# Block-sparse attention with a Fourier-mixing MLP: the first pair in two halves, and the last variances by ScalarE squares

## The chip, the cores and the metric

The kernel runs on one core of one Trainium2 chip. The metric is the device time of one execution in microseconds (us). A core has five engines that run side by side and hand work to each other through semaphores: TensorE (PE in the profile, with its weight loads as PEld), VectorE (DVE), ScalarE (ACT), GpSimd (POOL) and SyncE (SP), which here only issues transfers. Each engine works through its own list of instructions strictly in the order written. Matrix products land in PSUM; DVE and ACT carry them from there to SBUF.

## What is computed

Four batches, eight heads, 768 positions, head size 64. Attention first, in which a query sees its own block of 64 keys and the three blocks with the best gate scores; then a Fourier mix, a layer norm and an MLP over the 512 channels:

```
k_rep = k.reshape(B, H, n_blocks, 64, D).mean(axis=3)
gate_scores = einsum('bhsd,bhnd->bhsn', q, k_rep)        # causal blocks only
top_idx = argsort(gate_scores)[..., -3:]                 # plus the own block
scores = where(mask & causal, q @ k.T / sqrt(D), -1e9)
attn_out = softmax(scores) @ v
x = attn_out as (B, S, 512)
u = x + real(fft(fft(x, axis=1), axis=2))
mu, var = mean(u, -1), mean((u - mu) ** 2, -1)
un = (u - mu) / sqrt(var + 1e-06)
out = u + maximum(un @ w_ch1, 0) @ w_ch2
```

## The kernel before

Heads are taken in pairs: pair P (0 to 15) holds two heads, four pairs make a batch b (0 to 3). The order of all the work is written out by hand in one long string, ORDER. Each word of it is a step: its name, what it works on, and after an @ the number of the buffer slot that it allocates (for matrix products one of a few PSUM slots). A leading ~ moves a step to its second engine. Since the schedule is manual, each engine executes its instructions exactly in this order, and a step that waits holds back all that stands behind it on its engine.

The steps of a pair that matter here:

- Lq, Lk, Lv: the transfers of q, k, v from HBM, issued by SP. Pair 0's q and k are not in ORDER: consts_first issues them, one head on SP's queue, the other on ACT's.
- tq, tk: TensorE turns q and k, 128 positions at a time (a_tp, six transposes; for k of pair 0 four, and tj, b_tp, the other two). qc (a_q32) copies the turned q to SBUF in float32; qs (a_q) and kc (a_k) write the float16 copies that the scores use; ks (a_sums) adds up k over each block of 64.
- g, then gt, gu, gx, go, gl, gm: the gate scores and, on DVE, the top three of them and the mask. Pair 0 has a second set for the last 256 queries (gj, tg, xg, og, lg, mg), so that its first 512 can go ahead.
- s:P,i (s_mm): tile i of the scores; the mask is added by further matmuls at its end. e:P,i (s_exp): the exponential on ACT; d:P,i (s_sel): the causal edge on POOL. v: the product with v; x: its normalization into x_b on DVE.

The steps of a batch: the fold and the Fourier products (fs, fd, f, fe, y, ty, tr, m), then u:b,kp (m_u) on DVE, which adds x, writes two row tiles of u and their row sums into sm. For batches 2 and 3 (W7) follow bn:b,kt (n_stats: two DVE instructions per row tile give its mean and variance), nv:b,kp (n_guess: four small DVE instructions, a first guess of 1/sqrt(var) and the shift), xu:b,kp (m_x: one row tile scaled on DVE, the other on ACT, into x_b) and un:b,kp (t_copy: two transposing transfers, issued by SP, into unT). nr (n_newton, POOL) refines the guess for later use. w:b,it (w1_mm) is the first MLP product, whose first matmul reads columns 0 to 511 of unT; r its relu; c (w2_mm) the second product of batches 0 and 1, and T, S, p, po a seven-product form of it for batches 2 and 3. o and od finish and store a row tile.

At the very start consts_first also runs eight matmuls over a tile of zeros (warmps), before the first transposes.

Of the kernel before, what the change touches and what calls it, by code (L numbers as in the profile page):

```python
# [11 lines left out]
FP = mybir.dt.float32  # L12
F16 = mybir.dt.float16
# [99 lines left out]
d:0,1 Lk:5@2 s:1,3@0 gl:2 s:1,5@3 ~qs:4 tk:4@1 gt:3 gm:2@2 e:1,3 ~gu:3 v:0@2 d:1,4 ks:4 e:1,5 gx:3
kc:4 s:2,3@0 vc:1 go:3 x:0 s:2,0@3 e:2,3@0 Lv:3@0 s:2,4@1 d:1,5 d:1,3 e:2,0 g:4@2 gl:3 d:2,3 fs:0,1
Lv:2@1 tq:5@0 fs:0,0 e:2,4 gm:3@3 d:2,0 Lk:7@0 gt:4 d:1,0 tk:5@3 d:1,2 ~qc:5@1 d:1,1 s:2,5@2 ~kc:5
s:2,1@1 d:2,4 e:2,5 s:2,2@0 ~gu:4 e:2,1 vc:3 ks:5 v:1@2 e:2,2 qs:5 gx:4 s:3,5@1 go:4 s:3,0@3 gl:4
e:3,5@1 d:2,2 x:1 s:3,2@0 e:3,0 Lq:6@0 d:3,5 g:5@1 vc:2 e:3,2 s:3,3@2 gt:5 Lk:6@1 d:2,1 gm:4@0
s:3,1@3 d:3,0 gu:5 s:3,4@1 e:3,3 gx:5 d:2,5 v:2@0 d:3,2 kb:7 LT:0 e:3,1 W:0 Lq:7@1 fs:1,0 ~go:5
e:3,4 s:4,4@2 x:2 d:3,1 s:4,2@3 d:3,3 e:4,4@0 s:4,0@1 d:3,4 gl:5 v:3@0 fs:2,0 gm:5@1 e:4,2 fs:2,1
fs:1,1 e:4,0 s:5,2@2 x:3 s:4,5@3 e:5,2@1 s:4,1@1 fd:2,1 s:4,3@0 fs:3,0 e:4,5 s:5,3@2 fs:3,1 e:4,1  # L120
fd:2,0 s:5,5@3 fd:3,1 e:5,5 tq:6@1 fd:3,0 e:4,3 ~fe:0,3 s:5,0@3 f:0,2 e:5,3 tk:6@0 ~fe:0,0 ~fe:0,2
f:0,0 ~qc:6@0 s:5,4@2 LF:0 f:0,1 fe:0,1 ks:6 e:5,4 y:0,0@1 qs:6 Lv:4@0 f:0,3 e:5,0 Lc:0 pg:0 ks:7
d:4,0 g:6@2 d:4,1 ty:0,0 d:4,2 y:0,1@3 gt:6 Lv:5@1 d:4,5 ~tr:0,0 d:5,2 gu:6 gx:6 Lk:8@2 d:4,3
s:5,1@2 W:1 go:6 gl:6 ~tr:0,1 qc:7@1 m:0,2@1 vc:4 ty:0,1 gm:6@2 d:4,4 kc:6 m:0,0@3 d:5,0 u:0,2@0
d:5,4 e:5,1 Lk:9@1 d:5,3 v:4@0 qs:7 u:0,0@1 xu:0,2 s:6,4@1 xv:0,2 x:4 vc:5 m:0,1@2 kh:7 e:6,4@0
d:5,5 s:6,1@3 u:0,1@2 d:5,1 s:6,3@0 e:6,1 xt:0,2@1 ~xu:0,0 g:7@2 xv:0,0 ~xu:0,1 v:5@3 e:6,3 gt:7
un:0,2 ~gu:7 W:2 ~xv:0,1 xt:0,0@2 s:6,5@1 un:0,0 xt:0,1@0 e:6,5 s:6,0@1 un:0,1 Lq:9@2 s:6,2@2 e:6,0
x:5 w:0,8@0 d:6,0 bn:0,0 w:0,1@1 r:0,8 gx:7 kc:7 go:7 w:0,5@3 gl:7 gm:7@3 K:7 kb:8 w:0,6@0 r:0,5
ks:8 r:0,1 bn:0,3 w:0,3@3 r:0,6 d:6,3 bn:0,5 e:6,2 w:0,12@1 r:0,3 Lq:8@0 s:7,5@0 s:7,0@2 ~r:0,12
e:7,5@1 s:7,4@3 kh:8 e:7,0 s:7,3@0 fs:4,1 w:0,0@1 qc:9@0 e:7,4 Li:0 Lv:6@0 kb:9 e:7,3 w:0,10@2 qs:9  # L130
Lv:7@1 bn:0,1 r:0,0 s:7,1@3 Lk:10@0 r:0,10 ks:9 d:7,3 w:0,11@0 e:7,1 qc:8@1 s:7,2@1 kh:9 ~r:0,11
d:7,1 w:0,7@2 e:7,2 d:6,2 d:7,0 fs:5,1 d:6,4 ~qs:8 g:8@3 X:0 g:9@0 gt:8 w:0,14@1 gu:8 d:7,4 gx:8
r:0,7 d:6,5 ~go:8 kc:9 w:0,9@3 X:1 gl:8 gt:9 gu:9 gm:8@0 d:6,1 d:7,5 w:0,2@2 r:0,14 ~r:0,9 Lk:12@1
d:7,2 vc:7 ~vc:6 gx:9 w:0,13@0 K:8 kc:8 kb:10 w:0,4@1 ~r:0,13 r:0,2 ks:10 v:7@3 r:0,4 ~go:9 gl:9
gm:9@1 K:9 s:8,3@0 x:7 s:8,1@2 v:6@1 e:8,1@1 bn:0,2 e:8,3 s:8,0@3 x:6 d:8,1 w:0,15@2 e:8,0 fs:5,0
fs:6,1 s:9,4@0 fs:7,1 r:0,15 fs:7,0 s:8,2@1 fs:4,0 s:8,4@3 e:9,4@0 fd:7,1 c:0,0,0@2 fs:6,0 fd:6,0
# [60 lines left out]
def kernel(  # L197
# [34 lines left out]
    def pick(a, b):  # L232
        return b if other[0] else a
# [778 lines left out]
```

## Time and profile before

| | us |
|---|---|
| median of 3 runs (277.49 to 278.82) | 277.71 |
| the profiled execution | 277.79 |
| its span | 276.1 |
| TensorE busy | 267.9 |
| VectorE busy | 221.5 |
| ScalarE busy | 178.3 |
| GpSimd busy | 107.4 |

The span is what the trace covers; 1.7 us of the profiled execution lie around it. A row of the timeline gives the start, the duration, the engine, the line of the kernel, the operation, output <- inputs, the shapes and a count; in brackets stands how long the engine had been idle, and what released it. A row with a count above one is a run of instructions without a gap, from the start of the first to the end of the last. "SPq" and "ACTq" are the queues of transfers that SP and ACT issue; the duration there is that of the issue, not of the transfer. A row of the windows gives, for a stretch of time, the busy time of each engine in it. Matmuls overlap in the pipeline, so that a row of the timeline reaches past the start of the next one.

### The profile page before, as it was taken

To read this page: it belongs to the slowest core of one execution; us is meant where nothing else is said; L and a number is where in the kernel's file an instruction comes from. 1 tells how busy PE (TensorE), PEld (TensorE's weight loads), DVE (VectorE), ACT (ScalarE), POOL (GpSimd) and SP (SyncE) were. 2 spreads that over 40 slices of the span, in tenths; PEclk is the share of its full clock that TensorE was granted. 3 is DMA by queue.
4 is the path that set the end of the run, shared out by engine and by line. 5 is a ranking of instruction groups with operands and counts; after the bars stand their busy time and mean duration, and the time that the engine had idled before them with its cause. 6 is when DMAs were issued, how large, how long until landed. Compare 5 with 4: busy or idle time off the path is not lost.

```text
span 276.1 us, 7004 instructions
## 1 busy us (share of the span) xinstructions
PE 267.9 (97%) x2660; PEld 181.2 (66%) x2660; DVE 221.5 (80%) x683; ACT 178.3 (65%) x243; POOL 107.4 (39%) x304
## 2 busy tenths in 40 slices
PE   8899989999999999999999999999999999999995
PEld 4566766765576565666665755655766888666884
DVE  1888999998789889899789797879999894307883
ACT  3799999969999759978799687802546310274100
POOL 5155927634783476405976691520100011000000
PEclk9999999999999999999999999999999999999999
DMA  8999999998799999479471202351100412300025
GB/s 190 271 229 235 186 233 207 180 153 151 134 174 189 168 188 194 115 124 234 119 149 29 57 2 78 77 105 51 38 2 0 59 19 68 127 0 2 0 112 194
DMA packets 121138, 33.47 MB, mean 121 GB/s; under 512 B 113616, under 2 KB 118160, under 8 KB 121104
## 3 DMA queue, kind: packets, MB, share of 16 engines
q1 hardware_dynamic: 115872, 28.43, 48.1%
q0 software_dynamic: 3664, 4.19, 9.8%
q10 hardware_dynamic: 1568, 0.39, 0.6%
q8 instruction: 21, 0.34, 0.5%
q14 instruction: 13, 0.11, 0.1%
HBM read 28.55 MB, written 6.29 MB: 126 GB/s over the span
## 4 chain that ended last, share of the span: by engine, by line
PE 81%; DVE 6%; ACT 5%; POOL 2%; issue 2%; SPq 2%; DMA 1%; DVEq 0%; ACTq 0%; POOLq 0%
PE h L801 19%; PE cw L879 13%; PE c L820 12%; PE h L803 9%; PE sc L532 7%; PE av L567 5%; PE tp L320 2%; ACT pt L549 2%; PE yp L639 2%; PE sc L527 2%; PE mx L672 2%; SPq L742 2%; PE mx L673 2%; PE sc L539 1%; PE warmps L914 1%
## 5 line engine op out<-in xcount | busy, mean ns | idle before, releaser
L549 ACT ACTIVATE pt<-sc 128x1024 f16<-128x1024 f32 (+1 forms) x96 | 83.4, 925 | 12.1 <-PE sc L532 8.1
L801 PE MATMUL h<-unT,w 128*128 128x512 f16 x256 | 84.6, 379 | 0.3 <-DMA unT<-x 0.3
L803 PE MATMUL h<-unT,w 128*128 128x256 f16 x256 | 69.7, 272 | 0.0
L813 ACT ACTIVATE hT<-h 128x768 f16<-128x768 f32 x50 | 39.4, 811 | 41.1 <-PE h L803 40.7
L555 POOL TENSOR_SCALAR_AFFINE_SELECT pt<-pt 128x256 f16<-128x256 f16 x96 | 37.4, 413 | 21.0 <-ACT pt L549 19.9
L820 PE MATMUL c<-w_sb,hT 128*128 128x512 f16 x192 | 44.5, 379 | 0.0
L801 PEld LDWEIGHTS <-w 128*128 128x128 f16 x256 | 25.0, 98 | 29.7 <-issue 1.4
L820 PEld LDWEIGHTS <-hT 128*128 128x128 f16 x192 | 18.3, 98 | 20.3 <-issue 0.5
L253 POOL TENSOR_SCALAR_AFFINE_SELECT qk<-mt 32x160 f16<-32x160 f16 x72 | 23.9, 353 | 18.2 <-DVE mt L504 16.7
L803 PEld LDWEIGHTS <-w 128*128 128x128 f16 x256 | 25.0, 98 | 3.6
L532 PE MATMUL sc<-qk 96*128 96x512 f16 (+3 forms) x144 | 26.1, 305 | 0.0
L567 PEld LDWEIGHTS <-pt 128*128 128x128 f16 x672 | 22.3, 97 | 3.2 <-ACT pt L549 0.7
L567 PE MATMUL av<-v,pt 128*128 128x65 f16 x672 | 23.2, 193 | 0.3 <-ACT pt L549 0.3
L253 POOL TENSOR_SCALAR_AFFINE_SELECT qk<-q 64x768 f16<-64x768 f32 (+1 forms) x15 | 12.3, 822 | 22.8 <-ACT q L239 15.3
L886 DVE SCALAR_TENSOR_TENSOR u<-cw,rt,u 128x256 f32<-128x256 f32 x35 | 16.6, 480 | 4.7 <-PE cw L879 4.1
L879 PEld LDWEIGHTS <-s 128*128 128x128 f16 x192 | 18.8, 98 | 2.2
L532 PEld LDWEIGHTS <-qk 96*128 96x128 f16 x144 | 13.1, 98 | 7.8
L811 DVE TENSOR_SCALAR hT<-h 128x768 f16<-128x768 f32 x14 | 13.3, 956 | 4.0 <-PE h L803 3.9
L879 PE MATMUL cw<-w2t,s 128*128 128x256 f16 x144 | 16.4, 273 | 0.0
L250 DVE TENSOR_TENSOR s<-hT,hT 128x384 f16<-128x384 f16 x16 | 5.4, 354 | 13.4 <-ACT hT L813 13.3
L250 DVE TENSOR_TENSOR x<-av,rcp 128x768 f16<-128x768 f32 x16 | 15.3, 958 | 0.6
L879 PEld LDWEIGHTS <-hT 128*128 128x128 f16 x144 | 14.1, 98 | 2.0
(155 smaller groups left out, 457.2 us busy)
## 6 DMA issues: line engine op xcount, KB each, us to landing
nat<-in_v_dram SPq DMA_DIRECT2D x16, 384.0 KB, 4.6
out_dram<-u SPq DMA_DIRECT2D x20, 256.0 KB, 2.4
nat<-in_k_dram SPq DMA_DIRECT2D x36, 96.0 KB, 3.4
nat<-in_q_dram SPq DMA_DIRECT2D x36, 96.0 KB, 2.9
nat<-in_q_dram SPq DMA_DIRECT2D x13, 192.0 KB, 3.7
nat<-in_k_dram SPq DMA_DIRECT2D x13, 192.0 KB, 3.9
w_sb<-in_moe_w_ch_dram POOLq DMA_DIRECT2D x2, 1024.0 KB, 11.2
w<-in_moe_w_ch_dram POOLq DMA_DIRECT2D x2, 768.0 KB, 7.1
```

Of the source, the lines that this page charges most:

```text
L250: (eng or nc.vector).tensor_tensor(out=out, in0=in0, in1=in1, op=op)
L253: nc.gpsimd.affine_select(out=out, in_=in_, pattern=[[0, i] for i in n], base=0, channel_multiplier=0, compare_op=ALU.is_ge, fill=0.0)
L532: nc.tensor.matmul(ps[:, e, co:co + q1 - q0], qk[0:96, e, 1, 128 * jt:128 * jt + 128], qk[0:96, e, 0, q0:q1], start=True, stop=True)
L549: nc.scalar.activation(out=d["pt"][:, o:o + 2 * n].rearrange("p (e c) -> p e c", e=2), in_=d["sc", i][:, :, 0:n], func=AF.Exp, scale=0.125)
L555: nc.gpsimd.affine_select(out=dg, in_=dg, pattern=[[0, 2], [1, 128]], base=0, channel_multiplier=-1, compare_op=ALU.is_ge, fill=0.0)
L567: nc.tensor.matmul(av[:, e, 66 * st:66 * st + 65], pt[:, co:co + 128], vv[:, e, jt, 0:65], start=(cnt == 0), stop=(cnt == 20))
L801: nc.tensor.matmul(hp[:, 0:512], w1s, unT[:, dt, 0:512], start=(dt == 0), stop=(dt == NDT - 1))
L803: nc.tensor.matmul(hp[:, 512:768], w1s, unT[:, dt, 512:768], start=(dt == 0), stop=(dt == NDT - 1))
L813: nc.scalar.activation(out=hT, in_=hp, func=AF.Relu)
L820: nc.tensor.matmul(c_ps[b, g[0]][:, st - g[0], :], h_t[b, it][:, 128 * st:128 * (st + 1)], w2_sb[:, it, :], start=(it == 0), stop=(it == N ...
L879: nc.tensor.matmul(o, x, y, start=(i == 0 and W7_FIRST[n]), stop=(i == 7), skip_group_check=True)
L886: nc.vector.scalar_tensor_tensor(out=o, in0=c_ps[b, "w", st][:, W7_BANK[n], 0:256], scalar=rt_t[b][:, kt:kt + 1], in1=o, op0=ALU.mult, op1 ...
```

## The change

Start of the kernel:

- The loads of pair 0 go in two parts, rows 0 to 511 and rows 512 to 767, and k ahead of q. The four transfers of the first part are spread over SP and ACT as before, the four of the second part are all issued by SP.
- tq:0 now turns four row tiles; a new step tn:0 (b_tq) turns the other two. The float32 copy is split into ~qc:0 and ~qn:0 (b_q32), both on ACT; the float16 copy into qs:0, now on POOL, and ~qm:0 (b_q) on ACT.
- The zeros are a tile of their own, 128 wide, and are set first; seven warm-up matmuls instead of eight read it, four times over.
- TensorE's order for pairs 0 and 1 was "tq:0 tk:0 tj:0 g:0 gj:0 tq:1 tk:1 s:0,5 s:0,2 s:0,4 g:1 s:0,1 s:0,0 tk:2". It is now "tk:0 tq:0 tj:0 g:0 tn:0 gj:0 s:0,0 tk:1 s:0,2 tq:1 s:0,5 s:0,4 g:1 s:0,1 tk:2".
- DVE finishes the gate of the first 512 queries (gt gu gx go gl gm) before that of the last 256 (tg xg og lg mg); the two were interleaved. On ACT e:0,0 stands first of the exponentials, ahead of ~qc:1; it stood last of the first five, behind it. SP loads k of pair 1 before its q.

Batches 2 and 3: the six bn steps of each are gone. mn:b,kp (n_mean, DVE, one small instruction) turns the row sums into minus the mean, and sq:b,kt (n_square, ACT) squares a row tile of u with that as bias, and adds up the squares; its 512 results go into x_b, where xu overwrites them. nv takes the variance from these sums. On ACT the squares of batch 2 stand thus: "kc:15 sq:2,0 e:14,0 sq:2,4 e:14,1 sq:2,1 sq:2,5 e:14,2 e:14,4 ~vc:14 e:15,5 e:15,0 xu:2,2 e:15,3 e:14,3 xu:2,0 e:14,5 e:15,1 sq:2,2 e:15,2 sq:2,3 e:15,4 xu:2,1".

Elsewhere each engine has its steps in the order of before; many steps have other buffer slots.

```
-        two = P == 0 and who == 1
+        two = P == 0
...
+    def b_tq(P):
+        pairs[P]["tpn"] = ps = pst([128, 256], f"tpn_{P}")
+        src = nat[P, 0].rearrange("p st e d -> p st (e d)")
+        for st in range(4, NST):
+            nc.tensor.transpose(ps[:, 128 * st - 512:128 * st - 384], src[:, st, :], id32)
+
+    def b_q32(P):
+        conv(pick(nc.vector, nc.scalar), q_tile(P)[:, 512:S], pairs[P]["tpn"], None)
+
+    def b_q(P):
+        conv(pick(nc.gpsimd, nc.scalar), qk_s[P % NSLOT][:, 0, XW(P), 512:S], q_tile(P)[:, 512:S], [S - 512])
...
+    def n_mean(b, kp):
+        sm = st_t[b][2][:, 2 * kp:2 * kp + 2]
+        nc.vector.tensor_scalar(out=sm, in0=sm, scalar1=-1.0 / DM, scalar2=None, op0=ALU.mult)
+
+    def n_square(b, kt):
+        nc.scalar.activation(out=x_t[b][:, kt, :], in_=u_t[b, kt // 2][:, kt % 2, :], func=AF.Square,
+                             bias=st_t[b][2][:, kt:kt + 1], accum_out=st_t[b][0][:, kt, 1:2])
...
-            nc.vector.tensor_scalar(out=vr, in0=mv[:, :, 1], scalar1=1e-6, scalar2=None, op0=ALU.add)
+            nc.vector.tensor_scalar(out=vr, in0=ss, scalar1=1.0 / DM, scalar2=1e-6, op0=ALU.mult, op1=ALU.add)
...
-            nc.vector.scalar_tensor_tensor(out=nm, in0=mv[:, :, 0], scalar=-1.0, in1=g,
-                                           op0=ALU.mult, op1=ALU.mult)
+            tt(nm, nm, g, ALU.mult)
...
-        for who in (0, 1):
-            src = (q, k)[who]
-            t = npool.tile([128, NST, 2, 64], FP, tag=f"nat{who}{place[0]}", name=f"nat{who}_0", bufs=1)
-            nat[0, who] = t
-            for e, eng in ((0, nc.sync), (1, nc.scalar)):
-                eng.dma_start(t[:, :, e, :], src[0, e].rearrange("(st p) d -> p st d", p=128))
...
+        for h in (slice(0, 4), slice(4, NST)):
+            for who in (1, 0):
+                src = (q, k)[who]
+                for e, eng in ((0, nc.sync), (1, nc.sync if h.start else nc.scalar)):
+                    eng.dma_start(nat[0, who][:, h, e, :],
+                                  src[0, e].rearrange("(st p) d -> p st d", p=128)[:, h, :])
...
+        nc.vector.memset(wsrc, 0.0)
         nc.vector.memset(dummy, 1.0)
         nc.scalar.activation(out=dummy, in_=dummy, func=AF.Exp)
-        nc.vector.memset(wsrc, 0.0)
         wps = pst([128, 512], "warmps")
-        for _ in range(8):
-            nc.tensor.matmul(wps, wsrc[:, 0:128], wsrc, start=True, stop=True)
-        nc.vector.tensor_copy(out=dummy, in_=wps[:, 0:1])
-        nc.vector.tensor_copy(out=id16, in_=id32)
+        for _ in range(7):
+            nc.tensor.matmul(wps.rearrange("p (r c) -> p r c", c=128), wsrc, wsrc.rearrange(
+                "p (r c) -> p r c", r=1).to_broadcast([128, 4, 128]), start=True, stop=True)
```

More of the change, by code (lines that the diff above doesn't have):

```diff
@@ L113 @@
[L113 to L124, printed above, removed]
@@ new lines @@
+s:7,0@0 ~r:0,12 e:7,5@1 s:7,4@3 kh:8 e:7,0 s:7,3@1 fs:4,1 Li:0 qc:9@0 w:0,0@2 e:7,4 Lv:6@0 kb:9
+qs:9 Lv:7@1 e:7,3 w:0,10@0 bn:0,1 r:0,0 Lk:10@0 d:7,3 ks:9 s:7,1@3 r:0,10 w:0,11@1 qc:8@1 e:7,1
+s:7,2@2 kh:9 ~r:0,11 d:7,1 w:0,7@0 e:7,2 d:6,2 d:7,0 fs:5,1 d:6,4 ~qs:8 g:8@3 X:0 g:9@1 gt:8
+w:0,14@2 gu:8 d:7,4 gx:8 r:0,7 d:6,5 ~go:8 kc:9 w:0,9@3 X:1 gl:8 gt:9 gu:9 gm:8@0 d:6,1 d:7,5
+w:0,2@0 r:0,14 ~r:0,9 Lk:12@1 d:7,2 vc:7 ~vc:6 gx:9 w:0,13@1 K:8 kc:8 kb:10 w:0,4@2 ~r:0,13 r:0,2
+ks:10 v:7@3 r:0,4 ~go:9 gl:9 gm:9@1 K:9 s:8,3@1 x:7 s:8,1@0 v:6@2 e:8,1@1 bn:0,2 e:8,3 s:8,0@3 x:6
@@ new lines @@
+d:8,1 w:0,15@0 e:8,0 fs:5,0 fs:6,1 s:9,4@1 fs:7,1 r:0,15 fs:7,0 s:8,2@2 fs:4,0 s:8,4@3 e:9,4@0
+fd:7,1 c:0,0,0@0 fs:6,0 fd:6,0 e:8,4 fd:7,0 e:8,2 bn:0,4 s:9,3@1 s:9,1@3 Lq:10@1 fd:6,1 kc:10
+s:9,0@2 nv:0 c:0,0,1 ~fe:1,1 f:1,2 nr:0 f:1,3 e:9,3 f:1,1 ~fe:1,2 c:0,1,0 fe:1,0 f:1,0 Lv:9@1
+fe:1,3 kh:10 e:9,1 Lk:11@2 kb:12 e:9,0 s:9,5@1 c:0,1,1 ks:12 e:9,5 Lq:11@2 y:1,0@3 o:0,1 qc:10@0
+y:1,1@2 ~tr:1,0 o:0,0 Lq:12@0 qs:10 g:10@1 ~tr:1,1 c:0,4,0@0 gt:10 gu:10 kb:11 ty:1,0 d:8,2 d:9,5
+od:0,1 gx:10 ty:1,1 d:8,0 m:1,2@1 Lq:13@1 d:9,1 ~go:10 d:9,0 c:0,5,0 u:1,2@3 vc:9 d:8,3 gl:10
@@ new lines @@
+d:10,4 s:12,1@2 Lv:13@0 x:11 e:12,0@1 d:10,5 w:1,1@1 Lq:15@0 K:13 kc:14 ks:15 s:12,5@3 w:1,8@0
+gu:14 ~r:1,1 e:12,5 e:12,1 vc:15 gx:14 v:10@3 fs:11,1 r:1,8 Lv:12@1 d:12,1 fs:11,0 s:13,5@1
+s:13,3@2 x:10 e:13,5@0 w:1,11@0 e:13,3 d:13,5 fs:10,1 fd:11,1 s:13,1@1 r:1,11 fd:11,0 s:13,2@3
+fs:10,0 w:1,7@2 e:13,1 fd:10,1 go:14 fd:10,0 e:13,2 gl:14 s:13,4@0 f:2,2 w:1,3@1 ~fe:2,0 e:13,4
+gm:14@2 d:13,2 ~fe:2,3 f:2,3 d:13,1 kh:15 w:1,14@3 f:2,1 r:1,7 K:14 qc:15@1 s:12,4@0 r:1,14 ~fe:2,2
+f:2,0 w:1,0@2 e:12,4 nv:1 s:13,0@3 fe:2,1 ~r:1,3 y:2,0@0 e:13,0 ~r:1,0 d:13,0 s:12,2@1 d:13,3 pg:2
@@ new lines @@
+fs:13,0 d:14,4 s:14,5@0 m:2,1@1 o:1,4 e:14,5 d:14,1 od:1,4 s:15,1@2 d:15,5 u:2,1@1 s:15,2@0 d:14,3
+e:15,1 c:1,5,0 mn:2,1 d:15,1 sq:2,2 d:14,5 e:15,2 s:15,4@1 v:14@2 sq:2,3 d:15,2 e:15,4 nv:2,1
+c:1,5,1 ~xu:2,1 d:15,4 un:2,1 nr:2 v:15@0 o:1,5 T:2 c:1,2,0@1 x:14 od:1,5 un:2,0 c:1,2,1 x:15
+fs:12,1 fs:12,0 c:1,3,0 fs:14,1 fs:14,0 fs:15,1 fs:15,0 fd:14,1 fd:15,1 w:2,3@3 fd:14,0 fd:15,0
+c:1,3,1 f:3,0 r:2,3 fe:3,0 fe:3,2 f:3,3 w:2,15@2 o:1,3 f:3,1 od:1,3 w:2,11@0 S:2,3,2 r:2,15 o:1,2
+fe:3,1 T:0 od:1,2 w:2,7@3 ~r:2,11 y:3,0@2 r:2,7 S:2,3,0 S:2,7,2 f:3,2 w:2,2@1 ~tr:3,0 ~fe:3,3 T:1
@@ new lines @@
+y:3,1@0 pg:3 ~ty:3,0 r:2,2 w:2,10@3 T:3 ty:3,1 tr:3,1 m:3,0@1 r:2,10 m:3,1@2 S:2,2,0 u:3,0@3
+w:2,6@0 u:3,1 w:2,5@3 r:2,6 mn:3,1 mn:3,0 S:2,7,0 sq:3,3 w:2,8@1 r:2,5 sq:3,0 w:2,4@2 sq:3,1 r:2,8
+w:2,14@0 nv:3,0 sq:3,2 w:2,0@3 nv:3,1 r:2,14 S:2,3,1 S:2,6,0 w:2,12@1 S:2,2,1 r:2,0 S:2,3,3 S:2,5,2
+S:2,7,1 r:2,4 S:2,0,0 w:2,13@0 S:2,2,2 r:2,12 S:2,0,1 S:2,4,2 S:2,4,0 w:2,1@3 S:2,2,3 r:2,13
+S:2,6,2 S:2,4,1 S:2,0,2 S:2,6,1 w:2,9@2 r:2,1 xu:3,1 S:2,5,0 xu:3,0 p:2,0,2@1 S:2,0,3 S:2,6,3
+S:2,5,1 p:2,0,0@0 S:2,4,3 r:2,9 un:3,0 po:2,0,2 p:2,0,1@3 S:2,1,0 po:2,0,0 m:3,2@2 po:2,0,1 p:2,1,2
@@ L192 @@
+po:3,4,0 od:2,5 S:3,7,2 od:3,0 p:3,5,2 po:3,4,1 p:3,5,1 po:3,5,2 p:3,5,0 po:3,5,1 od:3,4,1 p:3,6,2
+po:3,5,0 od:2,3 od:3,3,1 p:3,6,1 po:3,6,2 od:3,5,1 od:3,1 p:3,6,0 po:3,6,1 od:3,5,0 od:3,4,0
+po:3,6,0 od:3,3,0
 """
@@ L277 @@
     gone = ctile([1, 4], F16, "gone")
-    wsrc = bpool.tile([128, 512], F16, tag="hT0", name="zeros")
+    wsrc = ctile([128, 128], F16, "zeros")
     nat = {}
@@ L327, in b_tp, with q_tile @@
             nc.tensor.transpose(ps[:, 128 * st - 512:128 * st - 384], src[:, st, :], id32)
+    def b_tq(P):
[7 more added lines that the diff above has]
+        conv(pick(nc.gpsimd, nc.scalar), qk_s[P % NSLOT][:, 0, XW(P), 512:S], q_tile(P)[:, 512:S], [S - 512])
+    def q_tile(P):
+        if "q32" not in pairs[P]:
+            pairs[P]["q32"] = apool.tile([128, S], FP, tag=f"q32{place[0]}", name=f"q32_{P}", bufs=1)
+        return pairs[P]["q32"]
     def b_sums(P):
@@ L407, in a_q32 @@
     def a_q32(P):
-        q32 = apool.tile([128, S], FP, tag=f"q32{place[0]}", name=f"q32_{P}", bufs=1)
-        pairs[P]["q32"] = q32
+        q32 = q_tile(P)
         if P in BLK[0]:
@@ L412, in a_q32 @@
         else:
-            conv(pick(nc.vector, nc.scalar), q32, pairs[P]["tp", 0], [S])
+            conv(pick(nc.vector, nc.scalar), q32 if P else q32[:, 0:512], pairs[P]["tp", 0], None)
     def a_q(P):
@@ L417, in a_q @@
         if P < NX:
-            conv(pick(nc.gpsimd, nc.scalar), qk[:, 0, XW(P), :], q32, [S])
+            n = S if P else 512
+            conv(pick(nc.gpsimd, nc.scalar), qk[:, 0, XW(P), 0:n], q32[:, 0:n], [n])
         else:
@@ L897, in consts_first @@
         npool.tile([128, 96], FP, tag="edge", name="edge")
-        for who in (0, 1):
-            src = (q, k)[who]
-            t = npool.tile([128, NST, 2, 64], FP, tag=f"nat{who}{place[0]}", name=f"nat{who}_0", bufs=1)
-            nat[0, who] = t
-            for e, eng in ((0, nc.sync), (1, nc.scalar)):
-                eng.dma_start(t[:, :, e, :], src[0, e].rearrange("(st p) d -> p st d", p=128))
+        for who in (1, 0):
+            nat[0, who] = npool.tile([128, NST, 2, 64], FP, tag=f"nat{who}{place[0]}", name=f"nat{who}_0",
+                                     bufs=1)
+        for h in (slice(0, 4), slice(4, NST)):
+            for who in (1, 0):
+                src = (q, k)[who]
+                for e, eng in ((0, nc.sync), (1, nc.sync if h.start else nc.scalar)):
+                    eng.dma_start(nat[0, who][:, h, e, :],
+                                  src[0, e].rearrange("(st p) d -> p st d", p=128)[:, h, :])
         nc.gpsimd.memset(wid, 1.0)
@@ L919, in consts_first @@
         nc.vector.memset(ltb, 0.0)
+        nc.vector.tensor_copy(out=id16, in_=id32)
+        nc.vector.tensor_copy(out=dummy, in_=wps[:, 0:1])
         nc.gpsimd.memset(indc, 0.0)
@@ L967 @@
         "m": m_mm, "u": m_u, "xu": m_x, "xt": t_mm, "un": t_copy,
-        "bn": n_stats, "nv": n_guess, "nr": n_newton,
+        "bn": n_stats, "mn": n_mean, "sq": n_square, "nv": n_guess, "nr": n_newton,
         "w": w1_mm, "r": w1_relu, "c": w2_mm, "o": w2_o, "od": w2_out,
```

130 lines of the change are left out of this document (55 added, 75 removed).

## The prediction

> **What bounds the kernel now.** I read the page's busy times first, then the engines' busy time by stretches, to find the stages in which TensorE has room, then the timeline of the two stages that the change touches.
>
> ```profile
> PE 267.9 (97%) x2660; PEld 181.2 (66%) x2660; DVE 221.5 (80%) x683; ACT 178.3 (65%) x243; POOL 107.4 (39%) x304
> ```
>
> ```profile
> 14.00:20.00 6.00, 6.00 (x76) 4.21 (x75) 5.21 (x20) 6.00 (x8) 3.27 (x8) 1.00 1.00 226
> 30.00:60.00 30.00, 28.63 (x497) 21.20 (x494) 28.47 (x96) 27.50 (x38) 16.84 (x38) 1.00 1.04 194
> 60.00:170.00 110.00, 109.70 (x1004) 68.20 (x1002) 94.80 (x302) 93.15 (x132) 64.74 (x180) 1.00 0.72 134
> 170.00:190.00 20.00, 19.73 (x178) 11.23 (x176) 16.68 (x43) 9.10 (x13) 6.66 (x22) 1.00 0.36 82
> 215.00:235.00 20.00, 20.00 (x180) 17.45 (x179) 14.87 (x41) 1.91 (x3) 2.54 (x11) 1.00 0.29 54
> ```
>
> The columns after the stretch are its length, PE, PEld, DVE, ACT, POOL. From 60 us on TensorE has work all the time; it is idle only 0.30 us in 60 to 170 and 0.27 us in 170 to 190. So from there whatever delays TensorE is lost for good, and whatever relieves another engine is worth nothing. Up to 60 us three engines are nearly full together (28.6, 28.5 and 27.5 of 30), and in 14 to 20 ACT has not a moment free: there a lead of the gate and ACT chain would count, and so would a lag. I take a shift of that chain at 15 us to reach 60 us whole.
>
> **Start of the kernel.** First TensorE's timeline, then three links of the chain of waits, ACT's timeline, DVE's last mask, and the median times from issue to landing.
>
> ```profile
> 1.31 3.59 PE L914 MATMUL warmps<-zeros 128*128 128x512 f16 x8 [1.31 <-DVE zeros L911]
> 4.69 2.34 PE L320 MATMUL tp<-id,nat 128*128 128x128 f32 x10
> 6.83 0.62 PE L327 MATMUL tpj<-id,nat 128*128 128x128 f32 x2
> ...
> 8.74 1.53 PE L320 MATMUL tp<-id,nat 128*128 128x128 f32 x12
> ```
>
> ```profile
> 7.14 0.70 DVE kra L390
> 7.98 0.51 PE g L433 x8
> 8.51 0.35 DVE gt L448
> ```
>
> ```profile
> 7.87 0.59 ACT L239 CAST qk<-tp 128x512 f16<-128x512 f32 x1 [0.85 <-DVE kra L390]
> ...
> 9.65 0.80 ACT L239 COPY q<-tp 128x768 f32<-128x768 f32 x1 [0.20 <-PE tp L320]
> 11.01 4.19 ACT L549 ACTIVATE pt<-sc 128x256 f16<-128x256 f32 x5 [0.55 <-PE sc L539]
> 15.06 0.83 ACT L239 COPY q<-tp 128x768 f32<-128x768 f32 x1
> ```
>
> ```profile
> 10.62 0.30 DVE L502 STREAM_TRANSPOSE mt<-lt 128x160 f16<-128x160 f16 x1
> ```
>
> ```profile
> nat<-in_q_dram ACTq DMA_DIRECT2D x1, 192.0 KB, 3.6
> nat<-in_k_dram ACTq DMA_DIRECT2D x1, 192.0 KB, 4.4
> ```
>
> The warm-up matmuls come every 0.42 us ((4.69 - 1.31)/8), the transposes of pair 0 every 0.214 ((6.83 - 4.69)/10), those of pair 1 every 0.11 to 0.13 (1.53/12): TensorE is at half speed at 6.8 us and at full speed at 8.7.
>
> Step by step after the change:
> - TensorE began at 1.31, released by the memset of the zeros; that is now a quarter as large and comes first. I take 0.2 us for it: seven matmuls from 1.1 end at 4.05 instead of 4.69.
> - Before, the first 384 KB (q) were there at 0.82 + 3.6 = 4.4 us, the next 384 KB (k, issued at about 1.3) at 5.7: 0.45 us per 128 KB. The first 256 KB (k) should thus be there at 3.95, the next (q) at 4.85.
> - So the four k transposes begin at 4.1, and the sums of k at 5.2 instead of 7.14. The q transposes wait for their load until 4.95; at 0.214 the four are done by 6.05 (the last takes some 0.42 to the end). The copy of 512 columns costs 0.59 (the cast of that size): 6.7. Then g:0 at 6.8 instead of 7.98: 1.2 us ahead.
> - g to the first gate transpose is 0.53 before (7.98 to 8.51), so 7.3 now. From there both halves together took until 10.92 (10.62 + 0.30), 2.4 us. The first half alone, by the same instructions, takes about 1.55 (8.85), so the first exponential comes near 9.2 instead of 11.01.
> - The second half needs another 1.35: its mask at 10.2, 0.7 ahead of 10.92. But TensorE now stands at s:0,2, whose mask matmuls want it, with tq:1 behind. Before, tq:1 ran at 8.74 while DVE was still at the gate. Now it runs after about 10.55, takes 0.9 to the end, and ACT copies pair 1's q at 11.45, not at 9.65. ACT is idle between e:0,0 (done by 10.2) and then.
> - ACT before: five exponentials from 11.01 to 15.06, 4.05 us. ACT now: from 11.45 the copy (0.80) and the other four (4.05 less 0.93): 15.4. At the same point of its list ACT is **0.3 us later** than before. The lead of 1.2 us at g:0 is spent on tq:1.
>
> Bounds: a lead of 1.8 (the first exponential's) if I am wrong about tq:1, a lag of 1.3 if TensorE stays at half speed up to that point. I take +0.3. SP issues four transfers more before pair 1's loads; at 0.45 to 0.57 us each these come some 2.2 us later in the queue, but pair 1's q is only turned at 10.55, and the queue was the transfers' backlog before: nothing, up to 0.7 if the cover fails. POOL, which has only memsets then, casts the first 512 of q in ACT's place; ACT's cast of the rest ends before the first exponential.
>
> **Batch 2.** The chain of waits runs through the last row pair of batch 2 (un:2,1, a store, un:2,0 on SP's queue, then the landing in unT), and TensorE waits for it:
>
> ```profile
> 174.74 1.31 DVE u L691 x4
> 176.06 0.62 DVE bst L747
> 176.88 0.59 DVE bst L747
> 178.52 0.56 DVE x L707
> 179.09 1.20 SPq L742
> 180.38 1.22 SPq L742
> 181.69 0.53 SPq L832
> 182.27 2.52 SPq L742
> 184.84 2.50 DMA unT<-x
> 187.47 0.38 PE h L801
> ```
>
> ```profile
> 177.71 0.17 DVE L759 TENSOR_SCALAR vr<-mv 128x2 f32<-128x2 f32 x1
> ```
>
> SP's queue has no gap from 179.09 on. Its first transpose begins when row tile 2 of x is there (178.52 + 0.56 = 179.08), the last landing releases w:2,3 at 187.47. So a delay of nv:2,1 (177.71) moves w:2,3 by as much.
>
> ```profile
> 163.35 4.02 ACT L549 ACTIVATE pt<-sc 128x1024 f16<-128x1024 f32 x4 [1.00 <-PE sc L532]
> ...
> 175.18 1.94 ACT L549 ACTIVATE pt<-sc 128x1024 f16<-128x1024 f32 x2 [0.68 <-PE sc L532]
> ```
>
> ```profile
> L727 ACT ACTIVATE x<-u,nm 128x512 f16<-128x512 f32 x7 | 4.9, 720 | 0.2
> ...
> L396 ACT COPY krb<-kr 64x12 f32<-64x12 f32 x18 | 3.6, 198 | 3.1 <-DVE kr L390 2.9
> ```
>
> ```profile
> 169.22 1.89 PE L820 MATMUL c<-w_sb,hT 128*128 128x512 f16 x8
> ```
>
> No square stands in the trace. Nearest is the ACT instruction of the same shape with a bias pointer, 0.72. Two exponentials take 1.94, one 1.02: back to back ACT saves 0.1 on each, so 0.62 is the lower end, with the sum read out free; with a read as long as ACT's smallest instruction (0.2) and no overlap it is 0.92, the upper end. I take 0.75, nearer to the row of its own shape.
>
> After: u:2,1 is done at 176.05, its mean at 176.25 (0.17 like nv's first). Then on ACT sq:2,2, e:15,2, which stands between the squares (0.93), and sq:2,3: ready at 176.3 + 0.75 + 0.93 + 0.82 = 178.8. nv:2,1 starts **1.1 us later** than at 177.71 (0.9 to 1.4), since the two batch-norm pairs that it replaces took 1.66 on an engine with nothing else to do. Behind the waiting nv:2,1 on DVE stands o:1,5, whose store is the one in SP's queue; it has to wait for TensorE anyhow.
>
> The four squares before put ACT back too: e:14,4 starts at 163.35 + 3 x 0.93 + 3 x 0.75 = 168.4 and ends at 169.4. Its PSUM slot (3) is now that of c:1,4,0, which TensorE reaches at 169.22: a stall of **0.2** (0 to 0.7), and all behind it moves.
>
> Together 1.3 (0.9 to 2.1). DVE is relieved of twelve batch-norm pairs; TensorE waits for none of them but these two, so that is worth nothing.
>
> **Batch 3.** The last transposes of unT and their user stand well apart:
>
> ```profile
> 215.43 14.35 SPq L742 DMA_TRANSPOSE unT<-x  x6
> ```
>
> ```profile
> 233.50 0.38 PE L801 MATMUL h<-unT,w 128*128 128x512 f16 x1
> ```
>
> Issued by 229.8, used at 233.5; ACT is busy 1.9 of 20 us there. Its squares are hidden behind 20 us of unbroken TensorE work; with a margin of some 2.5 us, cost 0.
>
> **Sum**: 277.79 + 0.3 + 1.3 = 279.4. The profiled execution is 0.08 above the median, which I neglect; I say 279.5.
>
> **Rivals.**
> - *A: forecast*, 279.5: squares on ACT in the wrong place, start a draw.
> - *B: the start's lead passes through.* Place: ACT's list at 9 to 15 us. ACT is what is full in 14 to 20, and its first exponential comes 1.8 us sooner; if q of pair 1 is copied before 10.2, no idle time follows e:0,0, and 1.8 of lead less 1.3 of batch 2 gives 277.3: not slower. Against it: tq:1 stands behind s:0,2. It decides if ACT's copy of pair 2's q starts at 14 or before instead of 15.06.
> - *C: batch 2 is covered.* One of SP's last two transposes takes 2.5 us where the others take 1.2; if that excess is a queue that drains on its own, a later start loses it again. Then only the stall is left: 277.79 + 0.3 + 0.2 = 278.3. Against it: the issues stand back to back.
> - *D: TensorE stays at half speed longer.* After the change TensorE has a first gap near 6.5 (before, its rows are unbroken to 6.83 + 0.62), in the time in which the speed rose before. If it rises only near 10.7, g, gj, tk:1 and two score tiles cost their time again, some 1.0 to 1.3: 280.6. The Trainium skill ("TensorE: Matmul & The Clock Gate", Part 1) says that the clock is doubled after a busy free-running window of about 3.4 us, whose phase differs from run to run, and (Part 4) that transposes count less towards it. By that rule seven matmuls (3.0 us here) fill no whole window, D would be the likelier and the time its 280.6. The trace agrees on a rise only long after the first matmul (between 6.8 and 8.7); but it came after 2 us of nothing but transposes, so here they did not hold it off.
>
> **How the numbers follow.** A 0.57, B 0.14, C 0.13, D 0.12, B with C 0.04 (276.5 or less). A change under 0.5% (1.4 us) is about what a measurement of this kernel cannot tell from none. A itself spreads over 278.5 to 280.8, and three quarters of it lie above 279.1; with D, 0.56 slower. B with C and a stronger B, 0.09 faster. The rest, 0.35, the same. The range, 277.3 to 281.2, goes from B to D with a slow square; A alone would be 278.5 to 280.8.
>
> **What would show it.** Right: g:0 near 6.8, the first exponential near 9.2, ACT idle about 1 us after it, ACT's copy of pair 2's q near 15.4; nv:2,1 over 1 us later against u:2,1; w:2,3 waiting 1 us or more for unT instead of 0.27. Wrong: that copy before 14.5 (B), w:2,3 waiting under 0.6 (C), transposes of pair 1 at 0.21 (D), a square at 0.6 or below, or a wait that I have not seen among the renamed slots between 15 and 60 us.

## The result and the profile after

The changed kernel takes 279.62 us (278.79 to 281.04) beside 277.97 us of the kernel before: a ratio of 1.006, with a 95% interval of 1.003 to 1.0089. The profiled execution took 279.40 us, its span is 277.6. The ratios here and below leave out executions over 1.5% above the fastest of their kernel (two of eleven with the squares side by side, one of eight with the second queue). First the busy times of the changed kernel, then some of its windows.

```profile
PE 267.5 (96%) x2659; PEld 179.8 (65%) x2659; DVE 213.9 (77%) x665; ACT 186.2 (67%) x268; POOL 109.1 (39%) x305
```

```profile
14.00:20.00 6.00, 5.44 (x71) 3.60 (x70) 5.50 (x21) 5.98 (x8) 3.86 (x9) 1.00 0.93 207
170.00:190.00 20.00, 19.02 (x174) 10.90 (x173) 15.32 (x40) 10.29 (x16) 7.78 (x22) 1.00 0.44 90
```

The work went over as it should: DVE has 7.6 us less, ACT 7.9 us more. TensorE has the same to do and is idle in new places: in 14 to 20 us it has lost 0.56 us, in 170 to 190 another 0.71.

Where the time comes in is read by following the same instructions through both chains of waits. From the kernel before (w:2,3 of that chain, at 187.47, stands in the prediction), then from the changed one:

```profile
33.40 1.39 PE av L567 x42
...
141.26 1.46 PE av L567 x42
...
255.34 17.48 PE cw L879 x160
```

```profile
15.11 4.50 DMA nat<-in_q_dram
19.74 0.86 PE tp L321 x6
...
22.24 5.42 DMA nat<-in_k_dram
...
34.18 1.39 PE av L585 x42
...
141.74 1.46 PE av L585 x42
...
188.71 0.38 PE h L826
...
256.57 17.48 PE cw L904 x160
```

At 33 us TensorE is 0.78 behind, at 141 only 0.48 (there the kernel before waits 0.30 for ACT, the changed one does not), at w:2,3 1.24, and then 1.23 to the end: batch 3 costs nothing. The rest of the 1.5 us between the spans lies behind the issue of the last store. The two loads in the chain, for pairs 4 and 5, were not there before.

Batch 2 in the changed kernel: DVE and ACT around the squares, then SP's queue and the MLP's first matmul.

```profile
176.50 0.08 DVE L709 DVE_READ_ACCUMULATOR u<-mx,x 128x1 f32 x1
...
179.28 0.17 DVE L785 TENSOR_SCALAR vr<-mv 128x2 f32<-128x2 f32 x1 [2.49 <-ACT x L768]
```

```profile
176.82 0.72 ACT L768 ACTIVATE x<-u,sm 128x512 f16<-128x512 f32 x1
177.44 0.19 ACT L768 ACTIVATION_READ_ACCUMULATOR x<-u,sm 128x1 f32 x1
177.54 1.00 ACT L567 ACTIVATE pt<-sc 128x1024 f16<-128x1024 f32 x1
```

```profile
180.66 2.50 SPq L760 DMA_TRANSPOSE unT<-x  x2
183.26 1.47 SPq L857 DMA_DIRECT2D out_dram<-u  x1
184.78 2.54 SPq L760 DMA_TRANSPOSE unT<-x  x2
188.71 0.38 PE L826 MATMUL h<-unT,w 128*128 128x512 f16 x1 [0.98 <-DMA unT<-x]
```

A square occupies ACT for 0.72 us (176.82 to 177.54, where the next instruction starts); its read-out of 0.19 is hidden. With the exponential between the two squares, nv:2,1 starts 2.70 us after the last sum of u:2,1 (179.28 - 176.58); before it was 1.66 (177.71 - 176.05). Behind it come SP's transposes, and w:2,3 waits 0.98 instead of 0.27.

### The profile page after: what moved, and what is told of

It is laid out like the page before. It is cut to its first block, busy times and chain, and to the rows that moved or that the text cites. A ratio compares the mean times of both kernels' runs of the same rounds, so it can differ in the third digit from the quotient of the medians.

```text
span 277.6 us, 7013 instructions
## 1 busy us (share of the span) xinstructions
PE 267.5 (96%) x2659; PEld 179.8 (65%) x2659; DVE 213.9 (77%) x665; ACT 186.2 (67%) x268; POOL 109.1 (39%) x305
## 4 chain that ended last, share of the span: by engine, by line
PE 83%; DMA 6%; ACT 4%; DVE 4%; issue 1%; SPq 1%; ACTq 0%; DVEq 0%
PE h L826 20%; PE cw L904 13%; PE c L845 13%; PE h L828 10%; PE sc L550 7%; PE av L585 7%; DMA nat<-in_q_dram 3%; PE yp L657 2%; ACT pt L567 2%; DMA nat<-in_k_dram 2%; PE mx L690 2%; PE mx L691 2%; PE sc L545 2%; PE tp L321 1%; PE g L459 1%
## 5 line engine op out<-in xcount | busy, mean ns | idle before, releaser
L845 PEld LDWEIGHTS <-hT 128*128 128x128 f16 x192 | 18.3, 97 | 20.4 <-issue 0.5
L254 POOL TENSOR_SCALAR_AFFINE_SELECT qk<-q 64x768 f16<-64x768 f32 (+2 forms) x16 | 12.9, 809 | 23.0 <-ACT q L240 15.1
L545 PE MATMUL sc<-qk 64*128 64x512 f16 (+3 forms) x112 | 14.9, 307 | 0.7 <-DVE qk L242 0.4
```

Source lines behind the costliest of these rows:

```text
L254: nc.gpsimd.affine_select(out=out, in_=in_, pattern=[[0, i] for i in n], base=0, channel_multiplier=0, compare_op=ALU.is_ge, fill=0.0)
L545: nc.tensor.matmul(ps[:, e, co:co + q1 - q0], qk[hs[e], 1, XW(P), 128 * jt:128 * jt + 128], qk[hs[e], 0, XW(P), q0:q1], start=(co == 0), s ...
L845: nc.tensor.matmul(c_ps[b, g[0]][:, st - g[0], :], h_t[b, it][:, 128 * st:128 * (st + 1)], w2_sb[:, it, :], start=(it == 0), stop=(it == N ...
```

## The experiments

Ratios are to the kernel before, with 95% intervals.

**The start alone.** The changed start and its PSUM slots; the statistics as before.

```diff
-            ss, g, nm, vr = [t[:, k] for t in (st_t[b][0][:, :, 1], *st_t[b][1:3], st_t[b][3][0])]
+            mv, g, nm, vr = [t[:, k] for t in (*st_t[b][0:3], st_t[b][3][0])]
...
-mn:2,1 d:15,1 sq:2,2 d:14,5 e:15,2 s:15,4 v:14 sq:2,3
+bn:2,2 e:15,2 d:15,1 d:14,5 bn:2,3 s:15,4
```

> The changed start (loads in halves, k first, halved transposes and q copies, seven warm-ups) alone; the last two batches' variances by batch-norm pairs in the order of before. Theory M, read from the trace after: the start has a lead of 0.3 us at pair 2's transposes, which is lost because the four extra issues on SP bring the loads of pairs 4 and 5 about 1 us later, so that TensorE waits for a load at tq:4 and again at a transpose of k near 27 us; it reaches the first w about 0.8 us later and, as GpSimd's wait near 141 gives 0.3 back, is 0.5 us late at 168: 278.5 us against 278.0 of before, and w:2,3 waits no more than the 0.27 us of before. Rival 1, the start is harmless and the lead of 0.3 lasts: 277.7. Rival 2, the lead is lost on ScalarE at pair 1's q copy, as the prediction has it: the copy of pair 2's q at 15.4 or later, 278.3.

Measured 278.34 beside 277.63: 1.0034 (1.0013 to 1.0054), 0.4 to 1.5 us. In its profiled execution TensorE waits for no load and passes 141 us at the time of before; the twelve times scatter from 277.6 to 280.7, those of before from 277.1 to 278.5. So theory M's waits are not in this trace, and the start does not cost the same in every execution. ScalarE's copy of pair 2's q comes at 14.94 in that execution, so Rival 2 falls as it was put (why this number moves between executions is told below); Rival 1 falls on the times.

**The squares alone.** The start of before, with the new statistics.

```diff
-bn:2,2 e:15,2 d:15,1 d:14,5 bn:2,3 s:15,4
+mn:2,1 d:15,1 sq:2,2 d:14,5 e:15,2 s:15,4 v:14 sq:2,3
```

> The start of before; the variances of the last two batches by the squares, in the changed order. Theory M: nv:2,1 starts about 1.0 us later against u:2,1, SP's transposes with it, and w:2,3 waits about 1.0 us for unT instead of 0.27; nothing else moves: 278.0 + 0.75 = 278.7 (278.5 to 279.1). Rival 1, the transposes' queue swallows the delay and the wait comes from the start's lag: 278.0. Rival 2, the four earlier squares delay the exponentials, so that TensorE also waits at c:1,4,0: 279.2 or more, with that wait in the trace.

Measured 278.41: 1.0030 (1.0019 to 1.0040). From this kernel's timelines:

```profile
178.20 0.17 DVE L767 TENSOR_SCALAR vr<-mv 128x2 f32<-128x2 f32 x1 [2.50 <-ACT x L750]
187.62 0.38 PE L808 MATMUL h<-unT,w 128*128 128x512 f16 x1 [0.96 <-DMA unT<-x]
```

The wait of 0.96 is there without the new start. Theory M's 0.75 us is inside 0.5 to 1.1; Rival 1 (nothing) falls, and Rival 2's further wait is not in the trace. The two parts add up: 0.34 and 0.30%, against 0.60 and (below) 0.64% together.

**The two squares side by side, and batch-norm for the last pair.** Two ways to take the delay of nv:2,1 away.

```diff
-mn:2,1 d:15,1 sq:2,2 d:14,5 e:15,2 s:15,4@1 v:14@2 sq:2,3
+mn:2,1 d:15,1 sq:2,2 sq:2,3 d:14,5 e:15,2 s:15,4@1 v:14@2
```

> The changed kernel with one step moved: the square of row tile 3 of batch 2 ahead of the exponential e:15,2, so that the two squares of the last row pair follow each other. Theory M (it is the exponential between the squares that makes nv:2,1 late): nv:2,1 comes 0.9 us earlier than in the changed kernel, w:2,3 waits 0.1 to 0.3 us, 279.6 - 0.75 = 278.9. Rival 1 (ScalarE's time as such): the exponentials e:15,2 and e:15,4 come late in turn, v:15 waits by what nv:2,1 gains: 279.6. Rival 2 (SP's queue is late for another reason, the landing does not follow nv:2,1): 279.6 with nv:2,1 early.

```diff
-mn:2,1 d:15,1 sq:2,2 d:14,5 e:15,2 s:15,4@1 v:14@2 sq:2,3
+d:15,1 bn:2,2 d:14,5 e:15,2 s:15,4@1 v:14@2 bn:2,3
```

> The changed kernel with the last row pair of batch 2 alone (row tiles 2 and 3) by the two batch-norm pairs on VectorE again; the other squares stay. Theory M: nv:2,1 is as late against u:2,1 as in the kernel before (1.66 us after it), w:2,3 waits about 0.3 us, 279.6 - 0.7 = 278.9, the same as with the two squares together. Rival (the other ten squares carry part of the cost): 279.3 or more, with a wait at c:1,4,0 or before w:2,3 that stays.

With the squares side by side 1.0056 (1.0037 to 1.0075), no gain that can be seen; with batch-norm 1.0034 (1.0022 to 1.0045), the gain that was expected, and no more than the start alone (1.0034): no cost of the other ten squares shows. In both nv:2,1 starts early, 1.8 and 1.66 us after u:2,1. SP's queue and the first matmul, first with the squares side by side, then with batch-norm:

```profile
178.97 0.17 DVE L785 TENSOR_SCALAR vr<-mv 128x2 f32<-128x2 f32 x1 [1.59 <-ACT x L768]
180.35 2.51 SPq L760 DMA_TRANSPOSE unT<-x  x2
182.95 0.53 SPq L857 DMA_DIRECT2D out_dram<-u  x1
183.53 4.77 SPq L760 DMA_TRANSPOSE unT<-x  x2
189.71 0.38 PE L826 MATMUL h<-unT,w 128*128 128x512 f16 x1 [1.38 <-DMA unT<-x]
```

```profile
179.60 2.50 SPq L760 DMA_TRANSPOSE unT<-x  x2
182.78 3.86 SPq L760 DMA_TRANSPOSE unT<-x  x2
188.55 0.38 PE L838 MATMUL h<-unT,w 128*128 128x512 f16 x1 [0.83 <-DMA unT<-x]
```

Here is what neither theory had: the way from the issue of un:2,1 to w:2,3 is not of fixed length. It takes 8.38 us before (179.09 to 187.47), 8.05 in the changed kernel, 8.04 with the squares alone, 9.36 and 8.95 here, and each time w:2,3 waits at its end. What nv:2,1 gains, the queue loses again in part. So "w:2,3 moves by as much as nv:2,1" holds only roughly. Rival 2 of the run with the squares side by side describes it; in the times batch-norm gained nonetheless.

**Three moves on the changed kernel**, beside that kernel itself as a control.

> The changed kernel itself, unaltered, as the control for the three kernels beside it on this chip. From the parts: the start alone cost 0.34% and the squares alone 0.30%, so 0.64% over the kernel before, about 1.8 us; if the parts hide each other, less than 0.5%.

The control gave 279.76 beside 277.89: 1.0064 (1.004 to 1.0087).

```diff
-                for e, eng in ((0, nc.sync), (1, nc.sync if h.start else nc.scalar)):
+                for e, eng in ((0, nc.sync), (1, nc.scalar)):
```

> The changed kernel with one difference: the second halves of head 1's k and q of pair 0 are issued on ScalarE's queue and not on SP's, so that SP issues two transfers fewer ahead of pair 1's loads (about 1.0 us at 0.5 us each). Theory M (the start's cost is that the later pairs' loads come behind the extra issues): the loads of pairs 4 and 5 are issued up to 1 us sooner, TensorE waits less for them, and about half of the start's cost goes: 0.2 to 0.4% over the kernel before, against about 0.6% of the changed kernel. Rival (the loads are late for lack of transfer rate, or the cost sits in the chain of ScalarE): no difference from the changed kernel. If ScalarE's two further issues delay its table load into its first copy, the gate scores come later than 6.0 us.

1.0039 (1.0024 to 1.0054). Lower than the control, as theory M has it, but the intervals overlap. Lk:1 is issued only 0.12 us earlier (3.84 instead of 3.96), not 1 us, Lv:1 0.7 (17.68 instead of 18.41).

```diff
-s:0,2@3 ks:1 tq:1@1 Lk:3@0
+tq:1@1 s:0,2@3 ks:1 Lk:3@0
```

> The changed kernel with one step moved on TensorE: pair 1's q transposes (tq:1) ahead of the score tile s:0,2, whose mask comes late. The prediction's reading (the lead at the gate is lost on tq:1, and ScalarE idles for 1.2 us after the first exponential): ScalarE copies pair 1's q about 0.6 us sooner, the copy of pair 2's q comes at 14.2 instead of 14.7, and 0.4 to 0.6 us are gained at the end. Theory M (the loads of pairs 4 and 5 set the end of this stage): the lead at pair 2 grows, but TensorE waits for the same loads at tq:4 and tk:5, and nothing is gained: 0.6% over the kernel before as in the changed kernel.

1.0044 (1.0029 to 1.0058), again inside the control's interval; the second run of this move, below, decides.

```diff
-un:2,1 nr:2 v:15@0 o:1,5 T:2 c:1,2,0@1 x:14 od:1,5 un:2,0
+un:2,1 nr:2 v:15@0 o:1,5 T:2 c:1,2,0@1 x:14 od:1,5
...
-od:1,4
+od:1,4 un:2,0
```

> The changed kernel with one step moved on SP's queue: the two transposing transfers un:2,0, whose input is ready at 175, ahead of un:2,1 and of the store od:1,5 (behind the store od:1,4, into the idle time of the queue before 180.6). Theory M (w:2,3 waits because the last row pair's delay pushes the store and un:2,0 along SP's queue, and they collide there with the fetch of instructions at 183 to 186): the last landing in unT is that of un:2,1, about 183 to 186 us; w:2,3 waits for it no more, 1.0 us is gained against the changed kernel: 0.2 to 0.3% over the kernel before. Rival (the transfers are slow as such near 184, whatever their order): w:2,3 still waits over 0.5 us for un:2,1.

1.0017 (1.0000 to 1.0033), 1.3 us below the control. SP's queue and the first matmul of this kernel:

```profile
175.40 7.12 SPq L760 DMA_TRANSPOSE unT<-x  x4
182.61 1.65 SPq L857 DMA_DIRECT2D out_dram<-u  x1
186.94 0.38 PE L826 MATMUL h<-unT,w 128*128 128x512 f16 x1
```

nv:2,1 is as late here as in the changed kernel (2.7 us after u:2,1), and w:2,3 has no wait at all. So the longer wait at w:2,3 was made in the order of SP's queue: un:2,0, ready since 175, stood last in it. The rival falls.

**The same move without the start.** On the kernel before, on the squares alone, and on the changed kernel together with the second queue; the diff is that of the move above, for the last one with that of the second queue.

> The kernel before with one step moved on SP's queue: un:2,0 ahead of un:2,1 and of the store od:1,5, as in e8. Theory M: the last landing is that of un:2,1 near 183 us, w:2,3 loses its wait of 0.27 us, and nothing else changes: 0.1% under the kernel before (0.0 to 0.2%). Rival (the order of the transfers matters only where the squares delay them): no difference, with the wait of 0.27 gone and another in its place.

> The start of before and the squares (as in e2), with un:2,0 ahead of un:2,1 and od:1,5 on SP's queue (as in e8). Theory M (the squares cost only through the delay of nv:2,1 into SP's queue): w:2,3 waits for nothing, and the whole 0.30% of e2 is gone, down to e9: 0.1% under the kernel before (between 0.15% over and 0.2% under). Rival (the squares cost elsewhere too): 0.2% or more over the kernel before.

> The changed kernel with both moves: the second halves of head 1 on ScalarE's queue (e5) and un:2,0 early (e8). Theory M: batch 2 costs nothing and gives the 0.27 us of before back; of the start stays what the chain of ScalarE lost, about 0.3 us, and a part of the loads' lateness: between 0.1% under and 0.2% over the kernel before, below e8. Rival (the halves' cost does not depend on SP's issues): the same as e8, about 0.2% over.

The kernel before with un:2,0 early: 277.01 beside 277.54, 0.9972 (0.9948 to 0.9995), the fastest version here and faster than both kernels; more than the wait of 0.27 us explains, but 0.1% is inside the interval. The squares with it: 0.9991 (0.9968 to 1.0014), in theory M's range, and w:2,3 waits for nothing; the rival's 0.2% lies outside the interval. But beside the kernel before with the same move they are still 0.6 us slower (277.61 against 277.01), where theory M had no difference. The two traces don't show where: from pair 2's first transpose to w:2,3 TensorE takes 173.7 us with the squares and 173.8 without. So the move takes the wait away, and whether the squares cost something elsewhere stays open. The changed kernel with both moves: 1.0013 (0.9997 to 1.0029), not told apart from 1.0017 with un:2,0 alone. Whether the second queue helps stays open.

**Pair 1's q first, with batch 2's wait gone.**

The changed kernel with the move of tq:1 and that of un:2,0, whose diffs stand above.

> The changed kernel with un:2,0 early (e8) and pair 1's q transposes ahead of the score tile s:0,2 (e6): with batch 2's wait gone, the start stands alone. The prediction's reading (the start is late because pair 1's q is turned behind s:0,2): the start's cost goes down by 0.3 to 0.5 us, to 0.0 to 0.05% over the kernel before, against 0.17% of e8. Rival (the later loads, or TensorE's order behind that point, set the end of this stage): no gain, 0.15 to 0.25% over.

1.0033 (1.0020 to 1.0046): no gain, as the rival has it. ACT's and TensorE's rows of this kernel:

```profile
10.44 0.80 ACT L240 COPY q<-tp 128x768 f32<-128x768 f32 x1 [0.44 <-PE tp L321]
...
15.03 0.80 ACT L240 COPY q<-tp 128x768 f32<-128x768 f32 x1 [0.51 <-PE tp L321]
```

```profile
11.73 0.39 PE L545 MATMUL sc<-qk 64*128 64x512 f16 x2 [0.72 <-DVE qk L242]
```

ACT's idle time before pair 1's q is 0.44 instead of 1.17, but TensorE now stands 0.72 us, instead of 0.39 in the changed kernel, at s:0,4. That tile takes PSUM slot 2 from tk:1 (in the kernel before, from tq:1, which ACT had copied by 10.45), and DVE frees it with kc:1, which comes after the second half's mask and ks:1:

```profile
9.31 0.31 DVE L394 STREAM_TRANSPOSE mt<-lt 128x128 f16<-128x128 f16 x1
9.56 0.96 DVE L408 TENSOR_REDUCE kr<-tp 128x12 f32<-128x768 f32 x1
10.43 0.95 DVE L242 CAST qk<-tp 128x768 f16<-128x768 f32 x1
...
11.44 0.39 PE L545 MATMUL sc<-qk 64*128 64x512 f16 x2 [0.39 <-DVE qk L242]
```

These are the changed kernel's. The row of the wait at s:0,4 stands in every trace with the changed start. Another slot for s:0,4 wasn't tried.

## Why the prediction was right, and where its parts were off

The forecast of 279.5 against 279.62 is right in the sum: 1.65 us instead of 1.7. Its two terms were both off, the start by some 0.6 us too little and batch 2 by 0.5 too much; that they cancel is luck.

*The start, +0.3.* The single steps came as drawn: g:0 at 5.99 to 6.63 (6.8 forecast), the first exponential at 8.69 to 9.33 (9.2), ACT idle 1.17 behind it (1), pair 2's q copied at 14.74 to 15.38 (15.4). The first number of each is the changed kernel's profiled execution, the second the control's; between them lies the clock, of which below. Pair 2's q copy in ACT's timeline, in the changed kernel and in the control:

```profile
14.74 0.80 ACT L240 COPY q<-tp 128x768 f32<-128x768 f32 x1
```

```profile
15.38 0.80 ACT L240 COPY q<-tp 128x768 f32<-128x768 f32 x1
```

Like with like, late clock against late clock, the copy is 0.32 us behind (15.38 against 15.06): here the size was right. The reason was half of it. In the changed kernel ACT has no gap from pair 1's q (10.88) to pair 2's (14.74), as drawn. But with tq:1 in front the copy comes just as long after g:0 (15.03 - 6.28 beside 14.74 - 5.99, both 8.75), since TensorE then stands at s:0,4 until DVE frees its slot: a second limit in the same place, a wait among the renamed slots, which the prediction looked for only between 15 and 60 us.

The step that failed comes behind it: "I take a shift of that chain at 15 us to reach 60 us whole", and from 60 us on every delay of TensorE was to be lost for good. In the kernel before TensorE waits in two places where the changed start, 0.3 us later, waits less or not at all:

```profile
20.56 0.69 PE L433 MATMUL g<-q,kr 64*32 64x288 f32 x8 [0.26 <-DVE qk L241]
...
141.26 1.46 PE L567 MATMUL av<-v,pt 128*128 128x65 f16 x42 [0.30 <-ACT pt L549]
```

The same instructions in the changed kernel with un:2,0 early, where the clock is late as well (at full speed from 5.78 by its record):

```profile
20.67 0.69 PE L451 MATMUL g<-q,kr 64*32 64x288 f32 x8
...
141.10 1.46 PE L585 MATMUL av<-v,pt 128*128 128x65 f16 x42
```

Its pair 2 begins 0.30 behind (13.71 against 13.41); 0.11 is left at 20.6, and at 141 it is 0.16 ahead. So it goes in the four of the ten traces with the changed start that have no other wait on the way (tq:1 in front, un:2,0 early, and both with the second queue): they pass the row of 141.26 at 140.83 to 141.15. ACT's lag is not what the start costs at the end.

What does is the step that was mis-sized, "the queue was the transfers' backlog before: nothing, up to 0.7 if the cover fails". It failed in part of the executions. Of the eight traces in which SP issues all the halves, four wait for q or k between 12 and 60 us, none of the four with the start of before does. From the waits of the changed kernel (us in total, times, longest):

```profile
PE tp L321 <- DMA nat<-in_q_dram: 0.6, 1, 0.6
PE tp L321 <- DMA nat<-in_k_dram: 0.5, 1, 0.5
```

With the squares side by side it is 0.3 and 0.6, with batch-norm for the last pair 0.6, with tq:1 and un:2,0 moved 0.2. The control has no such wait; there DVE stands before it turns a q, and TensorE behind it, which is 0.20 us late at 33 us and 0.76 at 61. From its chain of waits:

```profile
44.35 4.28 DMA nat<-in_k_dram
48.64 0.97 DVE q L428
```

The chain puts DVE's stand down to a load of k, though the step reads q; what held it is not shown. With the squares side by side it is there too. By the times the start costs 0.9 us (0.4 to 1.5). That the four extra issues make the loads late was argued from the queue and is not shown: neither run with the second queue had such a wait, but their times aren't told apart from those without it.

*Batch 2, +1.3.* nv:2,1 came 1.04 us later (1.1 forecast), a square took 0.72 (0.75). Two things were too much. The stall of 0.2 at c:1,4,0 did not come: that matmul follows on, 0.50 behind as TensorE was before it. And "a delay of nv:2,1 moves w:2,3 by as much" gave 1.1, where the wait grew by 0.71 and the way through the queue became 0.33 us shorter; that is rival C in part. By the times the squares cost 0.8 us (0.5 to 1.1).

*Batch 3, 0*, and "worth nothing" for the relief of DVE: right, the lag is 1.24 at w:2,3 and 1.23 at the end.

*The rivals.* B fell: the lead at pair 2 of the changed kernel's trace (0.32 us) is the early clock, and it was gone at the load of pair 4. D fell: no trace has pair 1's transposes at half speed, and TensorE is at full speed by 6.6 us in every trace of the changed start.

## What to carry to other kernels

Before pricing a delay, ask what stands last in the queue behind it, and whether it could stand earlier: here the transfer that TensorE waited for had been ready for 10 us, and moving it took that wait away and made the kernel before faster by 0.28%. A lead or a lag at the start of a kernel is to be followed engine by engine until something absorbs it, buffer slots, later loads and waits that were there before included. And one trace of a start is one draw: compare traces at the same phase of the clock.

## What was not expected of the hardware

**The clock's phase at the start.** TensorE's first rows in four executions: the changed kernel and its control, then the kernel with the squares alone (the start of before); that of before stands in the prediction.

```profile
1.07 3.03 PE L942 MATMUL warmps<-zeros 128*128 128x512 f16 x7 [1.07 <-DVE dummy L938]
3.94 1.37 PE L321 MATMUL tp<-id,nat 128*128 128x128 f32 x8
```

```profile
4.04 1.91 PE L321 MATMUL tp<-id,nat 128*128 128x128 f32 x8
5.75 0.64 PE L328 MATMUL tpj<-id,nat 128*128 128x128 f32 x2
```

```profile
4.40 0.82 PE L320 MATMUL tp<-id,nat 128*128 128x128 f32 x6
```

In the control the transposes come every 0.214 us ((5.75 - 4.04)/8), at half speed until after 5.75; in the changed kernel's execution and in the third they are fast from the first (six in 0.82). The same instructions rise in speed at 3.9 us in one execution and later than 5.9 in another, and with the start of before between 4.4 and over 7. The traces' records of the granted clock begin at the same places, at full speed: at 3.83 in the changed kernel, 6.58 in the control, 4.09 with the squares alone and 7.30 before (a page's PEclk takes the time ahead of the first record as full). That moves pair 2's q copy by 0.6 us in either kernel (14.74 and 15.38; 14.46 and 15.06). The Trainium skill ("TensorE: Matmul & The Clock Gate", Part 1) says that the window of activity runs freely, so that the number of slow matmuls differs from run to run. The traces agree; but it says that the first 3.4 us run at half speed and that the transition varies by 500 ns either way, where by these records full speed came 2.7 to 6.0 us after the first matmul in the traces of this case. The measurement decides.

**A transposing transfer's time.** Two transposing issues take 2.5 us, but 3.83 to 4.77 when they stand behind the store near 183 us; in other executions the store has the excess (1.47 instead of 0.53). The chain of waits of the changed kernel puts the store's excess down to DVE's reciprocal (done at 184.0); but with the squares side by side, where only one square stands elsewhere, the same store was issued at 182.95, ahead of that reciprocal (184.39), so it doesn't need it. In each trace one fetch of instructions on queue q8 and one on q14 lie in the same stretch (here the changed kernel, 182 to 186 us; the columns are packets, MB and share of 16 engines):

```profile
q8 instruction: 1, 0.02, 2.1%
q14 instruction: 1, 0.01, 2.0%
```

That they hold the transfers up was not tested.
